# Long convolution and soft MoE on one core: tables and zero fill loaded later and by SyncE, the tenth chunk's high rows ahead of the first filter unit

## The chip, the cores and the metric

The kernel runs on one core of one Trainium2 chip. The metric is the device time of one execution in microseconds. The engines are named PE (TensorE), DVE (VectorE), ACT (ScalarE), POOL (GpSimd) and SP (SyncE). SP computes nothing here; it issues DMAs in program order, and a DMA whose inputs are not ready holds every later one on SP. ACT can issue DMAs too, between its own instructions.

## The reference, cut to what matters

```python
Xf = np.fft.rfft(x, n=2*S, axis=1)          # x: 8 x 5696 x 128
Hf = np.fft.rfft(h, n=2*S, axis=0)          # h: 5696 x 128
y = np.fft.irfft(Xf * Hf[None], n=2*S, axis=1)[:, :S]
x = y.reshape(B*S, D)                        # 45568 tokens
logits = x @ phi                             # 32 slots
d = softmax of logits over all tokens;  slot_input = d.T @ x
slot_out = relu(slot_input[e] @ w1[e]) @ w2[e]   # 8 experts, 4 slots each
c = softmax of logits over the slots;   return c @ slot_out
```

## The kernel before, in words

The long convolution is a transform of length N1 x N2 = 90 x 64, made of matmuls with tables. There are nine sequences: the filter h is sequence 0, and the eight batches of x are 1 to 8. Each goes through the same stages, and stages of neighbouring sequences overlap.

- **loadx** (`load_x`, L183) brings a pair of chunks of the input into one of two buffers xc. Loads 0 to 3 are the filter's, 4 to 7 the first batch's. Load m waits until both folds of load m-2 have read its buffer. For loads 0 and 1 a third set of rows is loaded too.
- **fold** (L208) adds and subtracts the near and the far half on POOL, two instructions of 128x512 for each chunk (L216).
- **low**, **high** (`stage_a`, L229) multiply folded chunks with the table s1: 16 matmul records into two banks (L240), two evacuations on ACT (L242) into a buffer fst, of which there are four, and a store of 512 KB to the DRAM tensors fl or fh. The store is only queued in a list; **flush** (L222) issues what is in the list on SP (L224). One high stage serves two chunks: high9 takes the folds of chunks 8 and 9.
- **loadf** (`load_g`, L263) brings the rows of one unit from fl or fh into one of three buffers gt (L274). The rows come from all chunks of a sequence, so the first loadf of a sequence waits for the last low store to land. There are 12 units to a sequence.
- **forward** (`stage_b1`, L278) multiplies a unit with the table wt (L287); DVE then turns it (L306, L310). For the filter, DVE multiplies with the table turn and writes Hr and Hi. For the batches it multiplies with Hr and Hi (L306, L313).
- **backward** (`stage_b2`, L317) multiplies with the table vt (L328), ACT evacuates (L333), and stores to zm and zr are queued. The filter has no backward stage; the first one is backward12.
- **loadz**, **loadr** (L368, L381) bring zm and zr back for the output transform, with the tables im and ir (L414, L419); the first is product0. zr has 26 rows of a block of 32 that are written by the stores of backward. The other rows must be zero, and the zero fill before the first stage writes them, from the buffer zx that DVE sets to zero.
- The rest makes logits with phi, the two softmaxes, the experts and the output.

The order of the work is written out by hand: `run` (L638) goes through a string of stage names and calls each, and each engine executes its instructions in that order. All table loads stand before the first string: s1, phi, turn, im, ir and eight pieces of the zero fill (96 KB each, 24 rows of 4096 B) are issued by ACT, wt (1440 KB) and vt (1472 KB) by SP behind the first two filter loads. The diff touches L613 to L622, the table of stages at L628 and the first lines of the first string at L644 to L647.

Of the kernel before, what the change touches and what calls it, by code (L numbers as in the profile page):

```python
# [75 lines left out]
def kernel(  # L76
# [24 lines left out]
    nc = tc.nc  # L101
# [6 lines left out]
    N1, N2 = 90, 64  # L108
    R1, HALF, NP = S // N2, N2 // 2, N1 // 2
    CH = 4  # L110
# [9 lines left out]
    LOW, MAIN = HP, HP  # L120
    ctx.enter_context(tc.manual_schedule())

    t_s1, t_im, t_ir, t_w, t_v, t_turn = [
        nc.inline_tensor(t, f"tab_{n}").ap()
        for n, t in zip(("s1", "im", "ir", "w", "v", "turn"),
                        transform_tables(S, N1, N2, CH, LOW, MAIN))]
# [5 lines left out]
    zr = [nc.dram_tensor(f"zr_{b}", (2, 2, HALF, HALF, D), F32, kind="Internal").ap() for b in range(2)]  # L132
# [7 lines left out]
    phi = const.tile([D, NSL], F32, name="phi")  # L140
    im = const.tile([P, 2, HP], F32, name="im")
    ir = const.tile([P, HP], F32, name="ir")
# [25 lines left out]
    wt = fconst.tile([P, NP, HP], F32, name="wt")  # L168
    vt = fconst.tile([P, NU, 2, HP], F32, name="vt")
    turn = fconst.tile([P, 2, NW, 2, 2], F32, name="turn")  # L170
# [12 lines left out]
    def load_x(m, halves=((0, 2 * CH),)):  # L183

        if 2 * m >= (B + 1) * NJ:
            return
        g, j = divmod(2 * m, NJ)
        src = (x[g - 1] if g else h).rearrange("(a n) d -> a n d", n=N2)
        t_ = xcs[m % len(xcs)]
        last = slice(R1 - HALF, R1)  # L190
        sets = [(slice(0, P, 2), slice(0, HP)), (slice(1, P, 4), last)]
        if m < len(xcs):
            sets.append((slice(3, P, 4), last))
        for n0, n in halves:
            a = (CH * j + n0, N2 - CH * j - n0 - n)
            p = (n0, 2 * CH - n0 - n)
            for parts_, rows in sets:
                v, w = src[rows, a[0]:a[0] + n, :], t_[parts_, 0, p[0]:p[0] + n, :]
                nc.sync.dma_start(
                    out=bass.AP(tensor=w.tensor, offset=w.offset,  # L200
                                ap=[w.ap[0], [(2 * CH + p[1] - p[0]) * D, 2], [1, n * D]]),
                    in_=bass.AP(tensor=v.tensor, offset=v.offset,
                                ap=[v.ap[0], [(a[1] - a[0]) * D, 2], [1, n * D]]))
        xs[2 * m] = xs[2 * m + 1] = t_
# [151 lines left out]
    zring = [(ypool.tile([P, 2, CH, 2, D], F32, name="zc"), ypool.tile([P, 2, CH, D], F32, name="zx"))]  # L356
# [80 lines left out]
    def stage_c2(T, part=None):  # L437
        ks = (3, 1, 0, 2) if tail else (3, 2, 1, 0)
        for k in ks if part is None else ks[part:part + 1]:
            p = bank()  # L440
            for i in range(CH):
                nc.tensor.transpose(p[:, i * TR:(i + 1) * TR], ys[T][0:TR, k * CH + i, 0:D],  # L442
                                    ident[0:TR, 0:TR])
            nc.scalar.activation(yt[:, k * CH:(k + 1) * CH, :, :], of_tokens(p), AF.Copy)  # L444
# [165 lines left out]
    load_x(0, ((0, CH), (CH, CH)))  # L610
    nc.scalar.dma_start(out=s1[:, :, :], in_=t_s1)
    load_x(1)
    nc.sync.dma_start(out=wt[:, :, :], in_=t_w)  # L613
    nc.sync.dma_start(out=vt[:, :, :, :], in_=t_v)
    nc.scalar.dma_start(out=phi[:, :], in_=moe_phi)
    nc.scalar.dma_start(out=turn[:, :, :, :, :], in_=t_turn)
    nc.scalar.dma_start(out=im[:, :, :], in_=t_im)
    nc.scalar.dma_start(out=ir[:, :], in_=t_ir)
    for i in range(8):
        nc.scalar.dma_start(  # L620
            out=zr[i // 4][i // 2 % 2, i % 2, N1 - MAIN:].rearrange("k (j r) d -> (k j) (r d)", r=2 * CH),
            in_=zring[0][1][0:4 * (HALF - N1 + MAIN), :, :, :].rearrange("p h n d -> p (h n d)"))  # L622
    held = {}

    def load_w1(e_):
# [5 lines left out]
                  turn=stage_c2, part=lambda n: stage_c2(n // Q, n % Q), logits=stage_c3, maximum=column_max,  # L631
                  exponent=stage_c4, turnl=turn_logits, expd=exponents, tokens=stage_c5,
                  shift=softmax_shift, exp=softmax_exp, dispatch=dispatch, rowsum=softmax_sum,
                  scale=softmax_scale, weights=stage_c6, load=load_pair, loadz=load_main, loadr=load_rest)

    strides = dict(low=NJ, high=NJ, fold=NJ, loadf=NW, forward=NW, backward=NW, part=Q * NQ, flush=0)

    def run(words, batch=0):  # L638
        for word in words.split():
            name, n = re.fullmatch(r"([a-z]+)(\d*)", word).groups()  # L640
            stages[name](*[int(n) + batch * strides.get(name, NQ)] if n else [])

    run(
# [217 lines left out]
    for b in range(B):  # L861
# [6 lines left out]
        for n in cuts:  # L868
# [9 lines left out]
            for q in range(Q):  # L878
                dst = o_[:, 0:n, q, :]
                src = pq[q][:, 0:n * D].rearrange("p (k d) -> p k d", d=D)  # L880
# [4 lines left out]
            for m in (0, 1, 2):  # L885
# [3 lines left out]
                src = o_[:, ks[0]:ks[-1] + 1, :, :]  # L889
                if m:  # L890
                    t0 = group[ks[0]][0] * N2
                    nc.sync.dma_start(
                        out=ov[b, t0:t0 + len(ks) * RW * N2, :].rearrange(
                            "(w p n) d -> p w (n d)", p=P, n=m * CH),
                        in_=src.rearrange("p (w v) q d -> p w (v q d)", v=m))
                else:
                    nc.sync.dma_start(
                        out=ov[:, (R1 - 1) * N2:, :].rearrange("b (j n) d -> b j (n d)", n=CH),
                        in_=src.rearrange("p w q d -> p (w q d)"))
# [29 lines left out]
```

## Time and profile before

| | |
|---|---|
| time, median of 3 runs | 809.88 us (807.26 to 812.29) |
| the profiled execution: its own time | 807.44 us |
| the profiled execution: span from first to last instruction | 805.7 us |
| busy: PE, DVE, ACT, POOL | 714.2, 628.6, 428.7, 410.4 us |
| mean granted TensorE clock | 0.954 |
| moved by DMA | 282.49 MB, mean 351 GB/s |
| forward0's matmuls start | 51.89 us |

The page cuts the span into 40 slices of 20.1 us; each digit is the busy share of a slice in tenths. The view of stretches gives, for stretches that one chooses, the length, the busy time and the number of instructions of PE, PE's weight loads, DVE, ACT and POOL, and in the last three columns the granted clock, the DMA share (how much of the 16 DMA engines' time packets took) and GB/s. The chain of waits goes back from the last instruction, at each step to what released it; its columns are start, length and what ran. A DMA's step there lasts from its issue to its landing. The list of DMA issues gives the count, the size of one, and the median time from issue to landing.

### The profile page before, as it was taken

Reading aid. Unit: us, or ns where it says so; the run is one execution under the profiler, and the core shown is the slowest. Engines: PE = TensorE matmul, PEld = TensorE weight load, DVE = VectorE, ACT = ScalarE, POOL = GpSimd, SP = SyncE. Lnnn points to the kernel's source line nnn. Section 1 sums busy time; section 2 is a strip of 40 time slices with the busy share of each in tenths; the row PEclk is TensorE's granted clock in tenths of the full one; section 3 lists DMA queues with packets and bytes.
Section 4 is the critical chain, followed back from the end, with each engine's and each line's share of the span. In section 5 each row is a group of like instructions: output and inputs, shape, how many; then the busy total and the mean of one; then the engine's idle time right before and its main releaser. Section 6 shows DMA issues by size and latency. Waiting matters only on the chain.

```text
span 805.7 us, 21845 instructions
## 1 busy us (share of the span) xinstructions
PE 714.2 (89%) x8884; PEld 364.1 (45%) x8884; DVE 628.6 (78%) x895; ACT 428.7 (53%) x868; POOL 410.4 (51%) x368
## 2 busy tenths in 40 slices
PE   5867889769999999999999999999998887888892
PEld 1322233325444444554445445544444444356782
DVE  1029987748998999898999899999989996795542
ACT  2433345336666665666666666666565455474432
POOL 4655433324565666555666665566533533586000
PEclk9989999989999999999999999999999998999855
DMA  8999899999999999999999999999999898763998
GB/s 282 377 317 403 310 400 391 327 362 359 387 350 380 374 387 346 397 372 384 359 386 388 363 381 369 394 368 365 361 302 364 279 378 287 286 243 123 383 400 341
DMA packets 165930, 282.49 MB, mean 351 GB/s; under 512 B 9576, under 2 KB 129000, under 8 KB 160616
## 3 DMA queue, kind: packets, MB, share of 16 engines
q1 hardware_dynamic: 164824, 280.01, 96.5%
q8 instruction: 70, 1.15, 0.5%
q10 hardware_dynamic: 1008, 1.10, 0.4%
q14 instruction: 28, 0.23, 0.1%
HBM read 148.54 MB, written 132.53 MB: 349 GB/s over the span
## 4 chain that ended last, share of the span: by engine, by line
PE 52%; DMA 19%; DVE 16%; ACT 4%; POOL 3%; issue 2%; SPq 2%; ACTq 0%; DVEq 0%; POOLq 0%
PE bank L240 15%; PE bt L287 8%; PE bz L328 7%; DMA zx<-zr 6%; PE bank L414 6%; DMA out_dram<-o 5%; PE bank L419 4%; DVE yf L306 3%; DVE bt L306 3%; PE bank L442 3%; DMA fl<-fst 3%; POOL y L432 2%; PE bank L451 2%; DVE yf L313 2%; DMA xc<-in_h_dram 2%
## 5 line engine op out<-in xcount | busy, mean ns | idle before, releaser
L216 POOL TENSOR_TENSOR x<-xc 128x512 f32<-128x512 f32 x144 | 179.0, 1275 | 80.4 <-PE bank L240 56.6
L240 PE MATMUL bank<-x,s 128*32 128x512 f32 x1728 | 207.5, 604 | 12.6 <-POOL x L216 9.5
L242 ACT ACTIVATE fst<-bank 128x512 f32<-128x512 f32 x216 | 125.6, 595 | 82.3 <-PE bank L240 67.1
L287 PE MATMUL bt<-gt,wt 64*64 64x256 f32 x1620 | 117.2, 398 | 25.8 <-DMA gt<-fl 10.9
L333 ACT ACTIVATE zst<-bz 128x1024 f32<-128x1024 f32 x96 | 92.9, 968 | 79.2 <-PE bz L328 73.9
L432 POOL TENSOR_TENSOR y<-y,op 128x512 f32<-128x512 f32 x64 | 78.7, 1229 | 106.8 <-DVE op L406 104.3
L306 DVE TENSOR_TENSOR yf<-bt,Hi 128x1024 f32<-128x1024 f32 x96 | 112.4, 1171 | 16.4 <-PE bt L287 16.3
L313 DVE TENSOR_TENSOR yf<-bt,yf 128x512 f32<-128x512 f32 x192 | 119.3, 663 | 3.3
L240 PEld LDWEIGHTS bank<-x,s 128*32 128x32 f32 x1728 | 55.7, 111 | 127.3 <-issue 87.2
L306 DVE TENSOR_TENSOR bt<-bt,Hr 128x1024 f32<-128x1024 f32 x96 | 113.0, 1177 | 0.0
L328 PE MATMUL bz<-yf,vt 64*64 64x256 f32 x1440 | 98.8, 382 | 5.6 <-DVE yf L313 5.2
L287 PEld LDWEIGHTS bt<-gt,wt 64*64 64x64 f32 x1620 | 54.7, 135 | 87.8 <-issue 35.7
L528 POOL TENSOR_TENSOR L<-L,rs 128x512 f32<-128x512 f32 x32 | 33.6, 1050 | 109.0 <-DVE rs L523 99.6
L328 PEld LDWEIGHTS bz<-yf,vt 64*64 64x64 f32 x1440 | 54.1, 134 | 41.0 <-DVE yf L313 12.7
L432 POOL TENSOR_TENSOR y<-y,om 128x512 f32<-128x512 f32 x54 | 64.1, 1187 | 2.1
L422 ACT ACTIVATE y<-bank 128x512 f32<-128x512 f32 x32 | 19.1, 597 | 85.5 <-PE bank L419 85.5
L442 PE MATMUL bank<-ident,y 109*128 109x109 f32 x512 | 59.3, 261 | 3.3 <-DVE y L432 1.0
L414 PE MATMUL bank<-zc,im 64*64 64x512 f32 x480 | 60.3, 600 | 0.0
L442 PEld LDWEIGHTS bank<-ident,y 109*128 109x128 f32 x512 | 49.7, 141 | 12.9 <-issue 6.8
L306 DVE TENSOR_TENSOR yf<-bt,turn 128x1024 f32<-128x1024 f32 (+1 forms) x12 | 14.0, 1171 | 52.2 <-PE bt L287 52.2
L444 ACT ACTIVATE yt<-bank 128x360 f32<-128x360 f32 x128 | 52.5, 475 | 3.8 <-PE bank L442 3.7
L876 PE MATMUL op<-so,cT 32*128 32x128 f32 x704 | 45.9, 369 | 5.3 <-ACT o L884 4.7
(99 smaller groups left out, 856.2 us busy)
## 6 DMA issues: line engine op xcount, KB each, us to landing
fl<-fst SPq DMA_DIRECT2D x72, 512.0 KB, 7.9
gt<-fl SPq DMA_DIRECT2D x72, 512.0 KB, 7.1
zm<-zst SPq DMA_DIRECT2D x64, 512.0 KB, 9.3
zc<-zm SPq DMA_DIRECT2D x30, 1024.0 KB, 7.7
fh<-fst SPq DMA_DIRECT2D x36, 512.0 KB, 7.6
xc<-in_x_dram SPq DMA_DIRECT2D x32, 512.0 KB, 8.3
out_dram<-o SPq DMA_DIRECT2D x16, 1024.0 KB, 10.8
zx<-zr SPq DMA_DIRECT2D x30, 512.0 KB, 9.2
```

The lines of the kernel that those rows point to most:

```text
L216: nc.gpsimd.tensor_tensor(out=y_[:, o, :, :], in0=near, in1=far, op=AL.subtract if o else AL.add)
L240: nc.tensor.matmul(p[i * m:(i + 1) * m, :], s1[:, q + o, cols], columns(c_, o), start=True, stop=True)
L242: nc.scalar.activation(st[:, :, q, :], p[:, :].rearrange("p (n d) -> p n d", d=D), AF.Copy)
L287: nc.tensor.matmul(bt[q * HP:(q + 1) * HP, a, o, :], wt[r, 2 * i + q, :], t_[r, 2 * o + q, :, :].rearrange("p c d -> p (c d)"), start=True ...
L306: nc.vector.tensor_tensor(out=p_, in0=pv, in1=h_, op=AL.mult)
L313: nc.vector.tensor_tensor(out=y_[r, 0:k, c, :], in0=pv[:, :, c, :], in1=y_[r, 0:k, c, :], op=op_)
L328: nc.tensor.matmul(bz[a * HP:(a + 1) * HP, q, o, :], vt[r, i, a, :], y_[r, a * m + o, :, :].rearrange("p c d -> p (c d)"), start=True, sto ...
L333: nc.scalar.activation(zst[:, e_, 0:m, 0:n, :].rearrange("p o q x -> p q o x"), bz[:, 0:n, 0:m, :], AF.Copy)
L414: nc.tensor.matmul(ps[o, c][h_ * HP:(h_ + 1) * HP, :], im[r, c, :], zt[r, h_, :, c, :], start=True, stop=False)
L432: eng.tensor_tensor(out=part_, in0=part(v, 0), in1=o_[:, :, :], op=sign)
L442: nc.tensor.transpose(p[:, i * TR:(i + 1) * TR], ys[T][0:TR, k * CH + i, 0:D], ident[0:TR, 0:TR])
L444: nc.scalar.activation(yt[:, k * CH:(k + 1) * CH, :, :], of_tokens(p), AF.Copy)
```

## The change

Wt, vt and the tables that ACT loaded, except s1, are now loaded by SP, in three groups called from the string: vt and turn behind the filter's last load (loadx3), phi, im, ir and the zero fill behind the first batch's first load (loadx4), and wt behind the store of high7, ahead of low8. The zero fill is two DMAs of 96 rows of 4096 B (384 KB each) in place of eight of 24 rows; the DRAM side of each is four blocks of 24 rows. The stage high9 moves from behind forward0 and loadf3 to ahead of forward0; its store stays at the same flush, behind loadf3.

```diff
     load_x(1)
-    nc.sync.dma_start(out=wt[:, :, :], in_=t_w)
-    nc.sync.dma_start(out=vt[:, :, :, :], in_=t_v)
-    nc.scalar.dma_start(out=phi[:, :], in_=moe_phi)
-    nc.scalar.dma_start(out=turn[:, :, :, :, :], in_=t_turn)
-    nc.scalar.dma_start(out=im[:, :, :], in_=t_im)
-    nc.scalar.dma_start(out=ir[:, :], in_=t_ir)
-    for i in range(8):
-        nc.scalar.dma_start(
-            out=zr[i // 4][i // 2 % 2, i % 2, N1 - MAIN:].rearrange("k (j r) d -> (k j) (r d)", r=2 * CH),
-            in_=zring[0][1][0:4 * (HALF - N1 + MAIN), :, :, :].rearrange("p h n d -> p (h n d)"))
+
+    def load_tables(n):
+        for t_, src in (((vt, t_v), (turn, t_turn)), ((phi, moe_phi), (im, t_im), (ir, t_ir)), ((wt, t_w),))[n]:
+            nc.sync.dma_start(out=t_[...], in_=src)
+        if n == 1:
+            w = 4 * (HALF - N1 + MAIN)
+            for z_ in zr:
+                nc.sync.dma_start(
+                    out=z_[:, :, N1 - MAIN:].rearrange("o c k (j r) d -> (o c) (k j) (r d)", r=2 * CH),
+                    in_=zring[0][1][0:4 * w].rearrange("p h n d -> p (h n d)"))
...
     run(
-        "fold0 low0 fold1 loadx2 flush low1 fold2 fold3 flush high1 flush low2 loadx3 flush low3 "
-        "fold4 fold5 flush high3 flush low4 loadx4 flush low5 fold6 fold7 flush high5 flush low6 "
-        "loadx5 flush low7 fold8 fold9 flush high7 flush low8 loadf0 loadf1 loadf2 loadx6 flush "
-        "low9 fold10 fold11 flush forward0 loadf3 high9 flush low10 loadx7 flush forward1 loadf4 "
+        "fold0 low0 fold1 loadx2 flush low1 fold2 fold3 flush high1 flush low2 loadx3 tables0 flush low3 "
+        "fold4 fold5 flush high3 flush low4 loadx4 tables1 flush low5 fold6 fold7 flush high5 flush low6 "
+        "loadx5 flush low7 fold8 fold9 flush high7 flush tables2 low8 loadf0 loadf1 loadf2 loadx6 flush "
+        "low9 fold10 fold11 flush high9 forward0 loadf3 flush low10 loadx7 flush forward1 loadf4 "
```

More of the change, by code (lines that the diff above doesn't have):

```diff
@@ L633 @@
                   shift=softmax_shift, exp=softmax_exp, dispatch=dispatch, rowsum=softmax_sum,
-                  scale=softmax_scale, weights=stage_c6, load=load_pair, loadz=load_main, loadr=load_rest)
+                  scale=softmax_scale, weights=stage_c6, load=load_pair, loadz=load_main, loadr=load_rest,
+                  tables=load_tables)
     strides = dict(low=NJ, high=NJ, fold=NJ, loadf=NW, forward=NW, backward=NW, part=Q * NQ, flush=0)
```

## The prediction

> **What bounds the kernel now.** I read the page's 40 slices first, then the DMA issues, then stretches of 4 us, then the chain of waits and the order of time of the first 60 us, because everything that the diff moves lies there.
>
> ```profile
> span 805.7 us, 21845 instructions
> PE   5867889769999999999999999999998887888892
> DMA  8999899999999999999999999999999898763998
> ```
>
> From slice 9 to slice 29 (180 to 600 us) PE and DMA both stand at 9: the rest runs as fast as it can, so a shift at 180 us reaches the end as it is. The start is where both rows fall short.
>
> ```profile
> 0.00:4.00 4.00, 0.00 (x0) 0.00 (x0) 2.05 (x6) 0.00 (x0) 0.73 (x7) 1.00 0.54 131
> 4.00:8.00 4.00, 0.33 (x2) 0.19 (x4) 0.00 (x0) 0.00 (x0) 1.65 (x2) 1.00 0.77 212
> ...
> 12.00:16.00 4.00, 3.19 (x24) 0.82 (x28) 0.00 (x0) 2.39 (x5) 1.81 (x2) 1.00 1.01 382
> ...
> 44.00:48.00 4.00, 1.36 (x12) 0.13 (x4) 0.00 (x0) 1.08 (x2) 2.90 (x3) 1.00 0.72 253
> 48.00:52.00 4.00, 0.11 (x4) 0.11 (x8) 0.00 (x0) 0.00 (x0) 2.02 (x2) 0.53 0.74 226
> ...
> 88.00:92.00 4.00, 2.50 (x32) 0.87 (x24) 3.96 (x5) 1.37 (x3) 4.00 (x4) 1.00 0.45 151
> ```
>
> The last two columns are the DMA share and GB/s. From 12 to 44 us the share is about 1: transfers stand in one line, and each delays all behind it. It is short at the start, at 44 to 52 us (2.16 us of idle in the two rows) and around 88 us (2.64 us idle from 84 to 96).
>
> ```profile
> 40.81 6.79 DMA fl<-fst
> 47.60 0.02 SPq L274
> 47.62 0.04 issue
> 47.66 4.19 DMA gt<-fl
> 51.85 0.04 issue
> 51.89 1.98 PE bt L287 x16
> 53.87 4.17 PE bank L240 x32
> 58.05 1.07 PE bt L287 x16
> 59.11 0.02 issue
> 59.14 1.22 DVE yf L306
> ```
>
> The chain: low7's store lands at 47.60, only then SP issues the first load of the filter's rows, forward0 starts at 51.89. From 59.14 the chain is on DVE up to 95 us, 3.60 us a unit (L306 begins at 59.14 and 62.74). So the question is when gt for forward0 lands (T, 51.85 now), and how soon DVE then runs without a gap.
>
> ```profile
> 3.43 7.78 ACTq L620 DMA_DIRECT2D zr<-zx  x8
> 11.24 1.28 ACT L242 ACT_TABLE_LOAD   x1 [11.24 <-DMA xc<-in_h_dram]
> ...
> vt<-tab_v SPq DMA_DIRECT2D x1, 1472.0 KB
> wt<-tab_w SPq DMA_DIRECT2D x1, 1440.0 KB, 8.3
> ...
> zr<-zx ACTq DMA_DIRECT2D x8, 96.0 KB
> ```
>
> **Part 1: ACT freed.** Thirteen issues become one; ACT's first evacuation could come some 2.5 us earlier than 12.54 (low0's 16 matmuls run from 7.67 to 11.68, half of them fill the first bank by about 10, and the table load could be done). It saves nothing by itself: low0's store stands in the queue behind the third filter load (x2 below), whose transfer hides it. Bounds: 0 to 2.5 us gain; I take 0, the line of transfers being nearest.
>
> **Part 2: SP takes the issues.** Eight table and fill issues (wt and vt were SP's already), six of them new to SP, at 0.3 to 0.65 us: at most 3.9 us. Covered: up to 70 us SP sleeps 17.2 us waiting for ACT's fst and 4.8 us for fl. Without that cover, up to 3.9 us. POOL's queue issues no DMA here and is not passed. New waits: zx was memset by 1.9 us, the tables' buffers are fresh, so nothing is held. Needed first: turn at 53.9 (DVE), vt at 100.8, im at 162.9, ir and the zeros at 165 to 171, phi at 185; all land before 40, so nobody waits for them. wt is needed by forward0 and is counted in the line.
>
> **Part 3: the order of transfers.** I write the line down by landing times (the trace's semaphore counts). Before: the second h load lands at 16.2, wt 19.5, vt 23.4, x2 25.35, then stores about 1.35 us apart (low0 26.85, low1 28.03, high1 29.39), x3 31.23, ... low7 47.60, high7 48.95. So one store costs 1.35 us of the line, a later x load 1.9, vt 3.9, wt 3.8, gt 1.28.
> After, x0 and x1 share the engines with nothing but s1. Nine issues at the median 0.608 us end by 6.2, and with the shortest landing of such a load (3.4) x1 is there by 9.6, not 16.2. POOL's two folds for x0 (2.48 us each) end at about 10.8; x2 is issued then, and lands at 10.8 + 2.9 + 1.9 = 15.6 (2.9 is the gt load's 4.19 less its own 1.28). Behind it without gaps: low0, low1, high1 19.7; x3 21.5; vt and turn 25.6; low2, low3, high3 29.6; x4 31.5; phi, im, ir 31.8; the zero fill; low4, low5, high5; x5 (2.2); low6, low7, high7; wt; gt. Behind the fill stand 3 x 1.35 + 2.2 + 3 x 1.35 + 3.8 + 1.28 = 15.4 us.
>
> **The zero fill is the costly term.** Eight pieces of 24 rows become two of 96, whose DRAM side is four separate blocks of 24 rows. The trace counts which engines report: loads and stores with 128, 64 or 32 outer rows end with 16 updates, the 24-row pieces with 13 (one at once, then 12), and the last store of output line 897, 8 blocks of 16 rows, with 9 (one at once, then 8). So the outer count sets how many of the 16 engines work: 12 of 24, 8 of 8, and by these rows 4 of 4. A packet of 4096 B took 159 ns, so the fill costs now 8 x 24 / 12 = 16 packets, 2.5 us, on 12 engines, and the trace shows it: up to 49 us the last engine reports each transfer 2.1 to 2.9 us after the first; after the gap at 48 us 0.5 us. On 4 engines it is 2 x 96 / 4 = 48 packets, 7.6 us, and everything behind waits for these four. Bounds: 2.0 us (16 engines) and 7.6; I take 7.6, nearest to line 897's row, whose pattern is the same.
> [...]
>
> So gt lands at T = 31.8 + 7.6 + 15.4 = 54.8, which is 2.9 us later than now; with 2.0 it would be 49.2, 2.7 us earlier. (low7 lands at 48.4, and 48.4 + 4.19 = 52.6 is before 54.8, so wt hides the load's latency and fills the idle of 44 to 52 us.)
>
> **Part 4: high9 ahead of forward0.** Its 16 matmuls (1.9 us) need a bank that low8's evacuation frees; that waits for high5's store, about 43.5 in the new line, so high9 is done by 48 and does not hold forward0. Now forward1 comes 7.25 us after T's forward0 on DVE (59.14 - 51.89), because high9 and low10 (4.17) stand between. With low10 alone (1.92, or 2.1 at the slow clock) PE is ready and DVE sets the step: 53.94 - 51.89 + 3.60 = 5.65. Gain 1.6 us. PE's idle ahead of forward0 stays above 5 us, and after such idle the clock row reads 0.53 and forward0 takes 1.98 where others take 1.09; I keep 1.98. If the clock stayed up, 0.9 more is gained; the end of the range keeps it. If low10 found no bank the gain is 0.
> [...]
>
> **Sum:** +2.9 - 1.6 = +1.3 us. From 60 to 88 us DMA is full (1.04), and comes 2.9 late where DVE comes 1.3 late, but the idle of 2.64 us at 84 to 96 takes the difference. After that come links that wait for the last engine (fl 8.43 at 135.0, zr 7.44 at 158.0, zx 5.40 at 165.5); drained by then, they shift by 1.3 and no more. The profiled execution took 807.44 (span 805.7 and 1.7 around it): 808.7. The median of the runs, 809.88, is 2.44 above it: 811.2.
>
> **Rivals.**
> - *The fill is hidden or spread* (not slower than before). Place: x4's landing to low4's. If all 16 engines share it, T is 49.2 and the sum -2.7 - 1.6 = -4.3: 805.6. It decides from about 6 us of fill downward. For it: the eight pieces become larger. Against: line 897's count.
> - *The lag is not given back.* wt does not fit the hole, since the four engines' line never runs dry, and low10 finds no bank, so high9's move gives 0. Then the extra 7.6 - 2.5 = 5.1 us stands whole: 815.0. For it: DMA at 1.04 from 56 to 84. Against: the idle at 88 us, 0.45. If the store and load links at 132 to 171 also wait for the late engines, 3 us more.
> - *DMA idle all recovered*: the 2.16 and 2.64 us above and the 3.2 of the first 12 us: 801.9. Against: POOL's folds keep x2 from starting before 10.8.
>
> **How the numbers follow.** Forecast 0.60 (own range 808 to 814), fill hidden 0.19, lag kept 0.17, all idle recovered 0.04. About 1% (8.1 us) is what a measurement of this kernel can tell from no change: below 801.8 lies the last case and little of the second, 0.05; above 818.0 some half of the third, 0.08; within, 0.87. The range 804.5 to 816.0 reaches from the second case with the fast clock, 805.6 - 0.9, to the third with a spare us.
>
> **What would show it.** Right: the two fill DMAs end with 5 updates (one and four); from 32 us on the last engine reports some 7 us after the first; gt lands near 54.8; high9's matmuls come before 49; forward1's DVE work begins 3.60 after forward0's, not 5.20 (59.14 - 53.94); at 180 us everything is 1 to 2 us late. Wrong: 16 or 17 updates and gt near 49 (the second case), or an unfilled idle in DMA ahead of gt, or the zx wait at 165 to 171 us growing by more than 2 us.

## The result, and the profile after

| | before | after |
|---|---|---|
| median of 22 runs | 808.19 us (804.96 to 812.29) | 812.87 us (807.32 to 820.11) |
| ratio after / before | | 1.0059, 95% interval 1.0042 to 1.0075 |
| the profiled execution | 807.44 us | 807.57 us |

The kernel became 0.6% slower: 4.7 us by the medians, where 1.3 was forecast. The runs of the kernel after spread more than this difference, its first profile (820.11) was of a disturbed execution, and the second, shown here, is of the fastest of twelve, so totals are compared by ratios and traces by their stages. Its page:

```profile
span 805.7 us, 21836 instructions
PE   6658789779999999999999999999998788788892
DMA  8999999999999999999999999999999898763998
```

DMA's 8 in the fifth slice (80 to 100 us) has become a 9, and PE has lost in the second, third and fifth and gained in the first, fourth and ninth. The stretches:

```profile
0.00:4.00 4.00, 0.00 (x0) 0.00 (x0) 2.05 (x6) 1.28 (x1) 0.73 (x7) 1.00 0.53 135
4.00:8.00 4.00, 1.58 (x6) 0.37 (x10) 0.00 (x0) 0.00 (x0) 2.89 (x3) 1.00 0.83 225
8.00:12.00 4.00, 4.00 (x24) 1.76 (x20) 0.00 (x0) 1.19 (x2) 2.08 (x3) 1.00 0.67 216
...
32.00:36.00 4.00, 4.00 (x40) 1.00 (x32) 0.00 (x0) 0.60 (x1) 2.71 (x3) 0.98 0.85 262
36.00:40.00 4.00, 0.04 (x4) 0.00 (x0) 0.00 (x0) 0.00 (x0) 2.24 (x2) 0.87 0.73 240
40.00:44.00 4.00, 1.11 (x8) 0.46 (x12) 0.00 (x0) 1.58 (x4) 0.00 (x0) 0.50 0.85 277
44.00:48.00 4.00, 4.00 (x32) 1.13 (x28) 0.00 (x0) 1.78 (x4) 0.92 (x1) 0.78 1.07 360
48.00:52.00 4.00, 1.66 (x16) 0.27 (x8) 0.00 (x0) 2.17 (x4) 4.00 (x4) 1.00 1.02 366
52.00:56.00 4.00, 0.00 (x0) 0.00 (x0) 0.00 (x0) 0.00 (x0) 0.03 (x1) 0.58 0.99 361
```

There is a new hole at 32 to 44 us, exactly while the zero fill runs: four engines work on it, the DMA share falls to 0.73, and PE and ACT come to rest as well, since no buffer fst comes free (in the chain below, ACT's fst at 42.14 starts as low4's store lands). The idle of 44 to 52 us is filled now, as the prediction had it. The chain of waits shows the same:

```profile
31.24 10.80 DMA fl<-fst
...
42.14 1.09 ACT fst L242 x2
...
43.25 6.33 DMA fl<-fst
...
49.64 6.42 DMA gt<-fl
56.06 0.14 issue
56.20 2.02 PE bt L287 x16
...
58.23 1.23 DVE yf L306
```

low4's store takes 10.80 us behind the fill, and gt for forward0 lands at T = 56.06, 4.2 us later than before. The trace's semaphore events give the two fills 5 updates each, one at once and four later. The transfers around them:

| landing of | first engine | last engine | last engine, kernel before |
|---|---|---|---|
| ir, behind which the fill stands | 32.59 | 33.66 | |
| fill, its two DMAs | 36.07 | 40.68 | 16.0 |
| low4's store | 35.08 | 42.04 | 39.59 |
| high5's store | 40.07 | 44.97 | 42.30 |
| wt | 52.39 | 54.77 | 19.5 |
| gt for forward0 | 54.23 | 56.06 | 51.85 |

The last engine reports low4's store 7.0 us after the first. How far all this has brought the line of transfers by T is best read from long stretches. Kernel before, then after, each with 0 to 12 us, 12 to 40, and 0 to T:

```profile
0.00:12.00 12.00, 4.01 (x16) 0.91 (x16) 2.05 (x6) 0.76 (x1) 3.90 (x10) 1.00 0.73 199
12.00:40.00 28.00, 23.94 (x176) 8.95 (x176) 0.00 (x0) 12.12 (x22) 18.28 (x16) 0.94 1.04 386
...
0.00:51.90 51.90, 32.77 (x226) 11.08 (x226) 2.05 (x6) 16.96 (x29) 30.48 (x31) 0.93 0.92 318
0.00:104.00 104.00, 75.56 (x692) 26.50 (x692) 49.83 (x61) 34.71 (x58) 55.36 (x51) 0.95 0.95 340
```

```profile
0.00:12.00 12.00, 5.58 (x26) 2.13 (x30) 2.05 (x6) 2.48 (x3) 5.71 (x12) 1.00 0.68 192
12.00:40.00 28.00, 20.43 (x170) 6.41 (x162) 0.00 (x0) 10.53 (x18) 19.83 (x16) 0.92 0.95 324
...
0.00:56.10 56.10, 32.79 (x240) 10.40 (x240) 2.05 (x6) 18.55 (x31) 30.48 (x31) 0.88 0.90 301
0.00:104.00 104.00, 72.59 (x668) 24.81 (x672) 46.80 (x59) 34.08 (x57) 53.34 (x50) 0.92 0.94 330
```

Length times GB/s is what was moved: 51.9 x 318 = 16.5 MB before, 56.1 x 301 = 16.9 MB after. By T nearly the same has to be moved in both; the order only decides how fast. It went slower in the first 12 us and above all from 12 to 40.

DVE then shows the gain from high9. In the kernel before, forward1's work began 7.25 us after forward0's matmuls; now, in the order of time on DVE:

```profile
58.23 1.23 DVE L306 TENSOR_TENSOR yf<-bt,turn 128x1024 f32<-128x1024 f32 x1 [54.95 <-PE bt L287]
...
61.84 1.21 DVE L306 TENSOR_TENSOR yf<-bt,turn 128x1024 f32<-128x1024 f32 x1
```

61.84 - 56.20 = 5.64 us, where 5.65 was predicted. Against the kernel before, forward1 is 2.7 us late, and the DVE instruction that began at 180.3 us before is 3.2 us late.

This lag does not stay to the end of the trace. The same DVE instructions are 2.0 us late at 250 us, 2.1 late at 650, and 0.7 early at 700, and both profiled executions span 805.7 us. The first profile of this same kernel has no such step (11.9 us late at 650, 11.7 at 700), and the traces of high9 alone, the order alone and the fill first on four engines below have one of 2.7 to 2.9 us. So the step belongs to single executions. The traces show what the change does at the start; that the loss reaches the end is shown by the ratios alone.

### The profile page after: what moved, and what is told of

Same layout as the page of the kernel before. It is cut to its first block, busy times and chain, and to the rows that moved or that the text cites. A ratio compares the mean times of both kernels' runs of the same rounds, so it can differ in the third digit from the quotient of the medians.

```text
span 817.5 us, 21836 instructions
## 1 busy us (share of the span) xinstructions
PE 719.0 (88%) x8884; PEld 366.8 (45%) x8884; DVE 628.3 (77%) x895; ACT 429.3 (53%) x868; POOL 410.2 (50%) x368
## 4 chain that ended last, share of the span: by engine, by line
PE 53%; DMA 19%; DVE 14%; ACT 4%; POOL 3%; issue 3%; SPq 2%; DVEq 0%; ACTq 0%; POOLq 0%
PE bank L240 18%; PE bt L287 8%; DMA zx<-zr 7%; PE bz L328 7%; PE bank L414 5%; PE bank L419 4%; DMA out_dram<-o 3%; DMA fl<-fst 3%; DVE yf L306 3%; DVE bt L306 3%; POOL y L432 3%; PE bank L442 3%; DVE yf L313 3%; PE op L878 2%; PE bank L451 2%
## 5 line engine op out<-in xcount | busy, mean ns | idle before, releaser
L240 PE MATMUL bank<-x,s 128*32 128x512 f32 x1728 | 209.7, 620 | 18.4 <-ACT fst L242 10.9
L328 PE MATMUL bz<-yf,vt 64*64 64x256 f32 x1440 | 101.2, 389 | 5.4 <-DVE yf L313 5.0
L406 DVE TENSOR_TENSOR y<-bank,y 128x512 f32<-128x512 f32 x32 | 22.1, 690 | 37.9 <-ACT y L422 32.6
```

What stands on the lines that cost most here:

```text
L240: nc.tensor.matmul(p[i * m:(i + 1) * m, :], s1[:, q + o, cols], columns(c_, o), start=True, stop=True)
L328: nc.tensor.matmul(bz[a * HP:(a + 1) * HP, q, o, :], vt[r, i, a, :], y_[r, a * m + o, :, :].rearrange("p c d -> p (c d)"), start=True, sto ...
```

## The experiments

My theory after the result (A): the fill on four engines is the loss. Rivals: (B) the order itself, tables in front of the stores and loads rather than in the idle start; (C) the fill's place, whatever its engines; (D) high9 did not gain. Each ratio is to the kernel before, with its 95% interval; 0.1% is 0.8 us.

**The kernel after again**, without an edit, for a second profile and its size.

> The changed kernel unchanged, for a second profile and for its time beside the variants. Both theories: 1.006 of the kernel before (0.6% slower); the two fill DMAs end with 5 updates each, the second about 8 us after the tables ahead of it; forward0's rows land near 58.8 us.

Measured: 1.0052 (1.0031 to 1.0072). The loss is real; this is the profile shown above. Its T is 56.06; the 58.8 expected was that of the first profile (58.84), so that T of one kernel differs by 2.8 us between two executions.

**The fill on 16 engines**, at the same place, and **on 2**. The one writes 48 rows, outermost, with four blocks inside, the other makes four DMAs with two outer blocks. The source is shaped to match; those lines are left out here.

```diff
# fill_16
-                    out=z_[:, :, N1 - MAIN:].rearrange("o c k (j r) d -> (o c) (k j) (r d)", r=2 * CH),
+                    out=z_[:, :, N1 - MAIN:].rearrange("o c k (j r) d -> (k j) (o c) (r d)", r=CH),
...
# fill_2
+                for c in range(2):
+                    nc.sync.dma_start(
+                        out=z_[:, c, N1 - MAIN:].rearrange("o k (j r) d -> o (k j) (r d)", r=2 * CH),
...
```

> The changed kernel with the same two fill DMAs and the same bytes in 48 rows outermost (of 2048 B, four blocks inside), so that 16 engines share them. Theory A (the four engines' line is the cost): both fills end with 16 updates, cost about 2 us of the line and not 8, forward0's rows land some 6 us earlier than in the changed kernel (near 52.5), and the time is 5 to 6 us less: 0.998 to 1.000 of the kernel before. Rival B (the later tables and SP's issues are the cost, whatever the engine count): the rows land within 1 us of the changed kernel's and the time stays at 1.006.

> The changed kernel, its fill as four DMAs of two blocks of 24 rows, so that only two engines work on it: the suspected cost doubled, the bytes unchanged. Theory A: each ends with 3 updates, 96 packets of 159 ns on two engines, 15.3 us of the line instead of 7 to 8.5; forward0's rows land about 7 us later than in the changed kernel (56 to 59), at 63 to 66; time up by 3 to 7 us, 1.009 to 1.014 of the kernel before. Rival B (not the engines): within 0.1% of the changed kernel's 1.0055.

Measured: 1.0022 (0.9997 to 1.0047) on 16 engines, 1.016 (1.0125 to 1.0194) on 2. The updates are 16 and 16, and 3 for each of the four. From ir's landing to the fill's the line takes 2.5 us on 16 engines (34.3 to 36.76), 7.0 on 4, 14.1 on 2 (34.40 to 48.52); T is 52.93, 56.06 and 63.73. The stretches with 2 engines:

```profile
32.00:36.00 4.00, 4.00 (x32) 1.45 (x28) 0.00 (x0) 0.98 (x2) 1.92 (x2) 0.70 0.33 107
36.00:40.00 4.00, 0.88 (x11) 0.00 (x0) 0.00 (x0) 0.00 (x0) 3.03 (x3) 1.00 0.47 161
40.00:44.00 4.00, 0.00 (x0) 0.00 (x0) 0.00 (x0) 0.00 (x0) 0.00 (x0) 0.66 0.48 165
44.00:48.00 4.00, 0.00 (x0) 0.00 (x0) 0.00 (x0) 0.00 (x0) 0.00 (x0) 0.50 0.44 161
48.00:52.00 4.00, 1.27 (x8) 0.46 (x12) 0.00 (x0) 1.74 (x4) 0.00 (x0) 0.50 0.88 285
```

All compute engines stand still from 40 to 48 us. And with 16:

```profile
32.00:36.00 4.00, 4.00 (x24) 1.06 (x20) 0.00 (x0) 1.17 (x2) 2.13 (x2) 0.57 1.03 313
36.00:40.00 4.00, 3.04 (x32) 0.91 (x28) 0.00 (x0) 1.50 (x3) 2.82 (x3) 1.00 1.04 327
40.00:44.00 4.00, 4.00 (x43) 1.23 (x32) 0.00 (x0) 1.75 (x4) 0.00 (x0) 1.00 0.97 338
```

The hole is gone. What comes nearest to the price of the fill, by these two cases, is the idle of all 16 engines, one less the DMA share: 4 x (0.15 + 0.27 + 0.15) = 2.3 us with four engines, 4 x (0.67 + 0.53 + 0.52 + 0.56 + 0.12) = 9.6 with two. Against the kernel with 16, the ratios give 0.30 to 0.37% (2.4 to 3.0 us, by the two measurements of the kernel after) and 1.38% (11.1 us). So A holds for the engines: the interval on 2 engines lies above both of the kernel after. On 16 engines some two fifths of the loss seems left, where theory A gave none; that interval (0.9997 to 1.0047) holds both no loss and much of the whole.

**The fill alone**, in the kernel before: two DMAs of four blocks on ACT in place of the eight.

```diff
-    for i in range(8):
+    for z_ in zr:
         nc.scalar.dma_start(
-            out=zr[i // 4][i // 2 % 2, i % 2, N1 - MAIN:].rearrange("k (j r) d -> (k j) (r d)", r=2 * CH),
+            out=z_[:, :, N1 - MAIN:].rearrange("o c k (j r) d -> (o c) (k j) (r d)", r=2 * CH),
...
```

> The kernel before, its eight fill pieces alone replaced by the changed kernel's two DMAs of four blocks, still issued by ACT at the old place. Theory A: 48 packets on four engines in place of 16 on twelve, 5.1 us more in the line of these four, which nothing drains before 47 us: forward0's rows land at about 56 to 57 instead of 51.85, 1.005 to 1.006 of the kernel before. Rival B: six issues fewer on ACT and the same bytes: 1.000 or a little less.

Measured: 1.0043 (1.0022 to 1.0064). The merged fill slows the kernel before nearly as much as the whole change did. T is 53.95, 2.1 later than before, where 4 to 5 later was expected.

**high9 back** behind forward0 in the kernel after, and **high9 ahead alone** in the kernel before.

```diff
# high9_back, from the kernel after; high9_alone is the reverse, from the kernel before
-        "low9 fold10 fold11 flush high9 forward0 loadf3 flush low10 loadx7 flush forward1 loadf4 "
+        "low9 fold10 fold11 flush forward0 loadf3 high9 flush low10 loadx7 flush forward1 loadf4 "
```

> The changed kernel with high9 put back behind forward0 and loadf3. By the prediction's part 4 the step from forward0's start to forward1's work on DVE grows from 6.3 back to about 7.3 us and the time by 1 to 1.6 us: 1.007 to 1.008 of the kernel before. Rival: the units behind have slack and the time stays at 1.006.

> The kernel before with high9 ahead of forward0 and nothing else. Prediction's part 4: forward1's work on DVE begins 3.6 us after forward0's, not 5.2, and the time is 1 to 1.6 us less, 0.998 to 0.999 of the kernel before. Rival: high9 waits for a bank behind low7's store and holds forward0, or the later waits take it back: 1.000 or more.

Measured: 1.0072 (1.0052 to 1.0092) with high9 back, 0.9985 (0.9963 to 1.0007) with high9 ahead alone. Both say that high9's move gains 0.13 to 0.20%, 1.0 to 1.6 us; each interval alone reaches across no change. With high9 back, forward1's DVE work begins 5.63 us after forward0's DVE work, and 3.61 with it ahead; in the kernel before it is 5.20, and 4.14 with high9 ahead. So D falls at forward1, where the traces show the gain; that it reaches the end is likely and not shown.

**The order alone**: the kernel before, with its eight pieces on ACT and its high9, but the tables by SP at the places of the kernel after. The eight pieces then start on ACT at 1.96 us, where they started at 3.43 before, since no table stands ahead of them.

```diff
-    nc.sync.dma_start(out=wt[:, :, :], in_=t_w)
-    nc.sync.dma_start(out=vt[:, :, :, :], in_=t_v)
...
+        "loadx5 flush low7 fold8 fold9 flush high7 flush tables2 low8 loadf0 loadf1 loadf2 loadx6 flush "
```

> The kernel before with wt, vt and the small tables issued by SP at the changed kernel's places; the eight fill pieces stay on ACT ahead of the first stage and high9 behind forward0. This is the tables' order alone. Theory (DMA time that stands idle at the start, where only the filter's loads can be issued, is lost for good, and weighs against the idle filled at 44 to 52 us): between 1.000 and 1.004 of the kernel before, so that this, the fill's engines (0.33%) and high9 (-0.15%) add up to the change's 0.55%. Rival (the prediction's line without the four engines: forward0's rows 2.7 us earlier): 0.996 to 0.998.

Measured: 1.0013 (0.9995 to 1.003). By itself the order moves nothing that can be measured, at T = 51.62 for 51.85. It neither gains what I had worked out nor loses much: B is no more than a part of the loss.

**The fill late**: on 16 engines, issued behind high15's store, about 88 us.

```diff
-        "backward7 flush low15 fold16 fold17 flush forward9 backward8 high15 flush low16 loadf12 "
+        "backward7 flush low15 fold16 fold17 flush forward9 backward8 high15 flush zerorows low16 loadf12 "
```

> The changed kernel with the fill on 16 engines as in the earlier variant, issued behind high15's store where SP waits for low15's store and DMA stands idle (near 88 us). Theory A plus the line: 2.5 us of transfers leave the line ahead of forward0 (rows at about 50.5) and go into idle time: 0.998 to 1.000 of the kernel before. Rival: the line ahead of forward0 is not what sets the end, and it stays at the 1.002 of the variant with 16 engines.

Measured: 1.0045 (1.0024 to 1.0066), a miss: above the forecast and above the rival's 1.002. T came earlier, 50.58, and still the kernel is slower. I had taken the idle around 88 us for free room. The chain shows what it held:

```profile
88.67 7.94 DMA gt<-fl
...
96.74 1.99 PE bt L287 x16
98.73 4.22 PE bank L240 x32
102.95 1.07 PE bt L287 x16
104.05 1.23 DVE yf L306
```

The load of rows that stands behind the fill lands at 88.67 + 7.94 = 96.61, and the DVE work of forward13, which began at 101.03 before, begins at 104.05. Of these 3.0 us, 1.5 are the later start of forward12 (96.74 for 95.27), 0.9 its slower matmuls (1.99 for 1.09) after PE's wait for the rows, and the rest the slower low stage behind them (4.22 for 3.57). What is put there stands ahead of rows that are needed at once.

**vt and the small tables later**: wt with turn behind loadx3, vt behind loadx6, phi, im, ir and the 16-engine fill at 88 us. Three moves in one, so it tests only whether T is what counts.

```diff
-        for t_, src in (((vt, t_v), (turn, t_turn)), ((phi, moe_phi), (im, t_im), (ir, t_ir)), ((wt, t_w),))[n]:
+        for t_, src in (((wt, t_w), (turn, t_turn)), ((phi, moe_phi), (im, t_im), (ir, t_ir)), ((vt, t_v),))[n]:
...
+        "loadx5 flush low7 fold8 fold9 flush high7 flush low8 loadf0 loadf1 loadf2 loadx6 tables2 flush "
```

> The same, with wt and turn behind the filter's last load, vt behind the loads of the first three units, and phi, im, ir and the fill in the wait for low15's store. 3.9 us more leave the line ahead of forward0: its rows land at about 47 to 49, DVE starts 3 to 5 us earlier than in the kernel before, and what DMA must do by 100 us is unchanged: 0.995 to 0.998 of the kernel before. Rival: the units' loads then wait behind vt and DVE gets gaps: 1.000 or more.

Measured: 1.0104 (1.0068 to 1.0139), the other way from the forecast. T is 46.55, 5.3 us earlier than before, and forward1 starts 6.3 us earlier on DVE; by 101 us DVE is 4.5 us late. The chain tells where it went:

```profile
46.59 2.03 PE bt L287 x16
...
48.63 10.39 DMA gt<-fl
...
68.92 8.48 DMA gt<-fl
...
77.53 1.13 PE bt L287 x16
...
78.68 8.58 DMA gt<-fh
```

Where DVE set the step from 59 to 95 us in the kernel before, each unit now waits for its rows, which stand behind vt (landed at 55.05) and the stores. So T alone does not set the end: here, what was put off was paid for behind T. This refutes a reading that the prediction and my expectations shared.

**The fill first**: the kernel after, the fill by SP right behind loadx1, on 16 engines (its shape as in the one above) and on 4.

```diff
     load_x(1)
+    for z_ in zr:
+        nc.sync.dma_start(
+            out=z_[:, :, N1 - MAIN:].rearrange("o c k (j r) d -> (k j) (o c) (r d)", r=CH),
...
-        if n == 1:
```

> The changed kernel with the fill on 16 engines, issued by SP right behind the second filter load, where DMA otherwise stands half idle (share 0.50 at 8 to 12 us). Theory of the lost idle: the fill costs about nothing there, forward0's rows land some 2.5 us earlier than with the fill in the tables' group (52.9, so near 50.5), and the time is below both that variant (1.002) and the one with the fill at 88 us (1.0045): 0.998 to 1.000. Rival: as with the fill at 88 us, what leaves the line ahead of forward0 does not reach the end: 1.002 to 1.005.

> The changed kernel with its own two fill DMAs of four blocks (four engines), issued by SP right behind the second filter load: the fourth cell beside 4 and 16 engines at the tables' place and 16 at the start. Theory: the four engines' line (7.6 us) is longer than the idle of some 3 us at the start, so 4 to 5 us of it stay and forward0's rows land at 53 to 55; 1.002 to 1.005 of the kernel before, clearly above the 0.999 of 16 engines at the same place. Rival (only the place counts): 0.999 to 1.000.

Measured: 0.999 (0.997 to 1.001) on 16 engines, 1.0035 (1.001 to 1.0061) on 4, at T = 50.24 and 54.22; both as expected. With 16 engines at the start:

```profile
0.00:12.00 12.00, 5.15 (x32) 2.08 (x36) 2.05 (x6) 2.63 (x4) 5.67 (x11) 1.00 0.76 224
12.00:40.00 28.00, 23.44 (x190) 6.78 (x184) 0.00 (x0) 13.61 (x24) 19.85 (x16) 0.94 1.03 356
...
0.00:50.20 50.20, 31.84 (x240) 10.12 (x240) 2.05 (x6) 18.44 (x31) 30.48 (x31) 0.94 0.97 330
0.00:104.00 104.00, 76.27 (x712) 26.38 (x716) 52.63 (x64) 35.18 (x59) 55.36 (x51) 0.94 0.99 353
```

The same 50.2 x 330 = 16.6 MB are there at 50.24. The fill uses idle of the first 12 us: a share of 0.76, where the same fill at the tables' place left it at 0.63. The four kernels make a square:

| fill | at the tables' place | at the start | place |
|---|---|---|---|
| on 4 engines | 1.0052, 1.0059 | 1.0035 | 0.17 to 0.24% |
| on 16 engines | 1.0022 | 0.999 | 0.32% |
| engines | 0.30 to 0.37% | 0.45% | |

The engines (A) differ the same way at both places, at the start with intervals that just touch, and the runs on 2 engines and with the fill alone show them clear of noise. The differences of place (C) have the same sign twice, but each lies within its intervals, so that C, and that the two add up, is likely and not shown.

**The kernel before with high9 ahead and the fill on 16 engines**, two DMAs on ACT in place of eight.

```diff
+    zw = 8 * (HALF - N1 + MAIN)
+    for z_ in zr:
         nc.scalar.dma_start(
+            out=z_[:, :, N1 - MAIN:].rearrange("o c k (j r) d -> (k j) (o c) (r d)", r=CH),
...
-        "low9 fold10 fold11 flush forward0 loadf3 high9 flush low10 loadx7 flush forward1 loadf4 "
+        "low9 fold10 fold11 flush high9 forward0 loadf3 flush low10 loadx7 flush forward1 loadf4 "
```

> The kernel before with only high9 ahead of forward0 and the fill as two DMAs on 16 engines (ACT issues them at the old place, two for eight). The candidate for a version better than both: the tables keep filling the idle start, twelve engines lose 4 packets each (0.6 us), ACT is free some 5 us sooner. 0.996 to 0.998 of the kernel before. Rival: only high9 counts, 0.9985.

Measured: 0.9991 (0.9965 to 1.0017), where 0.996 to 0.998 was expected. With the two others at 0.9985 and 0.999 it is no slower than the kernel before; that any of the three is faster is not shown.

Across the runs, what DMA had moved by 104 us ranks the kernels nearly as the ratios do: 36.7 MB (0.999, fill first on 16), 36.3 (0.9991), 35.4 (before), 35.3 (1.0022, fill on 16), 35.2 (1.0013, order alone), 34.9 (1.0035, fill first on 4), 34.6 (1.0043, fill alone), 34.5 (1.0045, fill late), 34.3 (1.0052, after), 32.2 (1.0072, high9 back), 31.1 (1.016, fill on 2). Two stand out of the rank: high9 alone (35.2 at 0.9985), which moves no transfer, and the late vt (34.1 at 1.0104). I saw this after the runs, so it is a reading and no test; it rests on one execution of each kernel, and those of high9 back (819.11 us, median 813.64) and of the fill on 2 engines (823.01, median 819.25) are the longest of their kernels.

## Why the prediction was right or wrong

The forecast (within 1%, a little slower, 811.2 us) held, and the rival of the other sign fell. Two parts of the mechanism, the four engines and high9, were the ones forecast; the gain from the order did not come, and the size was off: +4.7 us for +1.3. That T came as near as 56.06 for 54.8 was in part luck: the engines were charged 2.5 us too much and the line 3.7 too little, and the two nearly cancel.

- *Four engines.* Right: 5 updates, 7.0 us of the line (33.66 to 40.68) for 7.6. The updates follow the outermost dimension in the other shapes too: 3 for 2 blocks, 16 for 48 rows.
- *"Everything behind waits for these four".* This is one mis-sized term. I charged 7.6 less 2.0, 5.6 us. Against 16 engines T is 56.06 - 52.93 = 3.1 us later and the ratios give 2.4 to 3.6. The other twelve engines work ahead on queued transfers (share 0.73 to 0.85, not 4/16), and the idle that is left, 2.3 us, is near that price.
- *"Behind it without gaps".* This is the other, with the opposite sign. My ledger fits the trace within 2.3 us: x1 at 11.85 for 9.6, x2 14.87 for 15.6, high1 19.3 for 19.7, ir 33.7 for 31.8, high5 45.0 for 43.5, gt 56.06 for 54.8. But with 16 engines T came at 52.93 for 49.2, and the kernel at 1.0022 (+1.8 us) where the sum gave -4.3. The order was to recover idle; it recovered that of 44 to 52 us, and gave back as much. The share of the first 12 us fell from 0.73 to 0.68, where SP has issued the filter's loads and one store alone, and on 16 engines too 12 to 40 us moved 341 GB/s for 386, which is 1.3 MB less. The order alone is +0.13%, where the sum without the four engines had a gain of 2.7 us.
- *Part 4, high9.* Right on DVE: 5.64 us for 5.65, a gain of 1.6. In the time it is 1.0 to 1.6 us by two runs, and neither difference is clear of no change. Its matmuls ended at 49.66 for 48, still 6.5 us ahead of forward0.
- *forward0 slow.* Right: 2.02 us for 1.98, where a later unit of the same trace takes 1.09, behind a row of 4 us (52 to 56) in which PE does nothing and the granted clock is 0.58.
- *"The idle of 2.64 us at 84 to 96 takes the difference".* Not borne out: DVE was 2.7 us late at forward1 and 3.2 at 180 us, where 1 to 2 was the sign given. The same three rows of 84 to 96 us still hold 2.0 us of idle (shares 1.00, 0.80, 0.70). That this idle was no free room is what the late fill showed.
- *zx.* Its wait did not grow: 4.90 us ahead of product0 for 6.11. The group of product0's and later matmuls, in the kernel before and after, with the idle before them and its cause at the end:

```profile
L419 PE MATMUL bank<-zx,ir 26*64 26x512 f32 x480 | 34.3, 628 | 9.6 <-DMA zx<-zr 9.6
```

```profile
L419 PE MATMUL bank<-zx,ir 26*64 26x512 f32 x480 | 34.3, 628 | 7.8 <-DMA zx<-zr 7.8
```

- *Parts 1 and 2.* No cost or gain of ACT's or SP's issues was seen. No run has them alone; in the order alone, which moves four of the six issues that SP gets, the sum of all effects is +0.13% with zero inside.

Put together from the runs: order +1.0 us, the fill's place +1.4 to +2.6, its engines +2.4 to +3.6, high9 -1.0 to -1.6: +3.2 to +6.2, and 4.2 to 4.7 were measured. Each term rests on ratios whose intervals reach 1.4 to 2.1 us to either side, so the sum agrees with the measurement and proves no term.

Open stays how much of the loss is the order and how much the fill's place. T came at 59.17 with high9 back, whose transfers up to there are those of the kernel after (56.06); but its profiled execution took 819.11 us, where its six others took 811.16 to 814.51, and the kernel after had 58.84 in its other profile. So T from a single trace is no better than some 3 us.

## What to carry to other kernels

Before merging small DMAs into one, look at its outermost dimension: here four blocks there meant four engines (5 updates), 48 rows brought 16 (16 updates), and between the two lay 2.4 to 3.6 us of time, near the 2.3 us of DMA idle with four. A transfer that was put off was paid for where it landed (the late fill, 1.0045; vt later, 1.0104), and the cheapest place found for the fill was the idle at the start, though that difference is not clear of the noise. An order is better judged by what has been moved by the end of the full stretch than by the landing of the first transfer that someone waits for: with vt later, rows came 5.3 us earlier and the kernel was 1.04% slower.

## What the runs showed of the hardware

The cost of few engines did not grow in line with the stretch that the fill took. From 16 engines to 4 the fill's stretch of the line grew by 4.5 us (2.5 to 7.0) and the time by 2.4 to 3.6; from 4 to 2 it grew by another 7.1 and the time by 8.2 to 8.7 (1.016 less 1.0059 and 1.0052). The ratio on 2 engines has four runs and a wide interval, but the traces say the same: the idle of all 16 engines is 2.3 us on 4 and 9.6 on 2. The transfers queued behind cover the first part (share 0.73 to 0.85 on 4, 0.33 to 0.48 on 2); then PE, without a free fst, makes no more (on 2 engines a store of 15.91 us lands at 49.89, and ACT's next fst starts at 49.99), and from 40 to 48 us no compute engine works. A full DMA share was not one rate: from 12 to 40 us the share was 1.04 at 386 GB/s before, 1.03 at 356 with the fill first.
